# A gated mix of a state-space convolution and an MLP: the last stage's adds move from DMA to VectorE, with named PSUM banks

## The chip, the core and the metric

The kernel runs on one core of a Trainium2 chip. The metric is the device time of one execution in microseconds (us); lower is better. TensorE (PE) multiplies, with its weight loads shown apart as PEld; VectorE (DVE) and ScalarE (ACT) work on tiles; GpSimd (POOL) and SyncE (SP) mostly issue DMAs here, and so does ACT at the end. Times below are counted from the start of the profiled span unless they are called durations.

## The reference

For 2048 tokens of width 512, the output mixes two branches of the same input with a gate per token:

```python
x = A_u
g = _sigmoid((x * gate_w).sum(-1, keepdims=True))
a = _A_ref(x, ...)   # long convolution (state-space kernel K), by FFT, plus u * Dskip
b = _B_ref(x, ...)   # gelu(x @ w1 + b1) @ w2 + b2, hidden width 1792
return g * a + (1 - g) * b
```

The convolution kernel K is built from complex exponentials of 512 x 128 parameters, and the convolution over 2048 positions is done by transforms.

## The kernel before, in words

The program has two parts, `front` and `conv`. `front` runs the whole MLP branch, builds the convolution taps and does the first stage of both transforms. A planner orders its work. It ends at about 426 us and leaves in memory: `tu_d` (signal after the first stage), `tk_d` (taps after the first stage), and in the output tensor `out` the finished MLP part (1-g)·b of 14 of the 16 tiles of 128 tokens. The last two tiles (14 and 15) hold only half of their MLP sum there; the other half is added in `conv` (`rest`, L1176, 21 groups of three matmuls, and L1228).

`conv` (L1073 on) is written out in order by hand (a manual schedule: each engine runs its instructions in the order of the program). It has two stages.

**The loop of 16 steps (L1200 to L1220).** Step `s` works on two of 32 frequencies. It issues the loads that later steps need: taps tiles `tk` (L1089, two of 256 KB a step up to step 10, each first used by `taps` five steps later in numbering and about two steps later in time), matrices `cc` (L1086), and in steps 4 to 6 signal tiles (L1205). VectorE forms the complex product (`product`, L1126), PE does the next step's signal transform (`signal`, L1119, into PSUM tiles `p2u` under the tag `pu`) and the taps transform of the step after that (`taps`, L1110), then the inverse transform of the product (`inverse`, L1138, tag `pa`). `turn` (L1149) copies the two results with ScalarE into two of six staging tiles `sa` and stores each (256 KB, L1155, on SP's queue) to the scratch tensor `t4_d`, which the profile writes `t_d`. After every fourth step (3, 7, 11 and 15) the eight finished rows are fetched back by four DMAs of 512 KB (L1163) into the tiles `den` and `t3` (written `t`), turned so that the last stage can use them. I call these four DMAs a gather. The first three gathers are issued by GpSimd, the last by ScalarE. A gather waits until all stores of its four steps have landed.

After steps 12 and 13 the loop also loads two of the eight pairs of output tiles, pairs 6 and 7, from `out` into `mos[6]` and `mos[7]` (L1220, 512 KB each, SP's queue). `room` (L1167) says where a pair lies: in places of `attic` and `loft` whose signal tiles have been used by then.

**The last stage (L1223 to L1257).** Four warming matmuls (`warm`, two records each in the profile) come first. Then, for eight pairs `m` of output tiles, PE does two matmuls for each tile `pb` (L1236; in the profile each matmul is two records). A pair's two tiles are allocated together, from the tag `pu` with four buffers or, for pairs 2 and 5, the tag `pa` with two. The first matmul needs the first DMA of all four gathers (`den`). For pairs 0 to 5 VectorE scales the first tile by the gate (L1250) and ScalarE the second (L1248), and GpSimd issues a DMA of 512 KB that adds the pair to `out` in memory (L1255, `accum_op`). For pairs 6 and 7 VectorE scales and adds to the loaded `mos` tile (L1246), and plain stores follow (L1257 on SP; L1252 on SP and ScalarE, 256 KB each).

SP's queue is in order. In the built program each of its DMAs also waits for an earlier one to land: eight semaphores are used in turn, so a DMA waits for the one eight places before it.

Of the kernel before, what the change touches and what calls it, by code (L numbers as in the profile page):

```python
# [9 lines left out]
F32 = mybir.dt.float32  # L10
# [3 lines left out]
ALU = mybir.AluOpType  # L14
# [3 lines left out]
P = 128  # L18
L = 2048
D = 512  # L20
# [254 lines left out]
def gated_mix(  # L275
# [18 lines left out]
    nc = tc.nc  # L294
# [14 lines left out]
    gate = cp.tile([P, 2, 16], F32, name="gate")  # L309
# [763 lines left out]
    def conv(pool, ps, late, attic, loft, den):  # L1073
# [8 lines left out]
        def fetch(n):  # L1082
            if n % 4 == 0:
                m = n // 4
                cc = pool.tile([P, 384], F32, tag="cc", name=f"cc{m}", bufs=4)
                nc.sync.dma_start(cc, c2[m])  # L1086
                c4s[m] = cc
            t2s[n] = pool.tile([P, D], F32, tag="tk", name=f"tk{n}", bufs=N_TK)
            nc.sync.dma_start(t2s[n], tk_d[ko[n]])  # L1089
# [12 lines left out]
        def pair(s, r, c, out):  # L1102

            for i in range(2):
                n = 2 * s + i
                w = mats[n // 4][0][c][:, n % 4]
                x = t2s[n] if r else us[n]
                nc.tensor.matmul(out[64 * i : 64 * i + 64], w, x, start=True, stop=True)  # L1108

        def taps(s):  # L1110
            fac[s] = []
            for c in range(2):
                pk = ps.tile([P, D], F32, tag="pk", name=f"p2k{s}{c}", bufs=2)
                pair(s, 1, c, pk)
                k = pool.tile([P, D], F32, tag=f"k{c}", name=f"k{s}{c}", bufs=2)
                nc.scalar.copy(k, pk)  # L1116
                fac[s].append(k)

        def signal(s):  # L1119
            pus[s] = []  # L1120
            for c in range(2):
                pu = ps.tile([P, D], F32, tag="pu", name=f"p2u{s}{c}", bufs=4)
                pair(s, 0, c, pu)
                pus[s].append(pu)

        def product(s):  # L1126

            (ur, ui), (kr, ki) = pus.pop(s), fac.pop(s)
            v = [pool.tile([P, D], F32, tag=f"v{i}", name=f"v{s}{i}", bufs=2) for i in range(2)]
            nc.vector.tensor_mul(v[0], ur, kr)  # L1130
            nc.vector.tensor_mul(v[1], ur, ki)
            nc.vector.tensor_mul(zs[0], ui, ki)
            nc.vector.tensor_mul(zs[1], ui, kr)
            nc.vector.tensor_sub(v[0], v[0], zs[0])
            nc.vector.tensor_add(v[1], v[1], zs[1])
            prod[s] = v

        def inverse(s):  # L1138

            v = prod.pop(s)  # L1140
            for i in range(2):
                n = 2 * s + i
                pas[n] = ps.tile([P, D], F32, tag="pa", name=f"pa{s}{i}", bufs=2)
                r = slice(64 * i, 64 * i + 64)
                w = mats[n // 4][1][r, s % 2]
                for c in range(2):
                    nc.tensor.matmul(pas[n][64 * c : 64 * c + 64], w, v[c][r], start=True, stop=True)  # L1147

        def turn(s):  # L1149

            for n in (2 * s, 2 * s + 1):
                sa = sas[n % 6]
                nc.scalar.copy(sa, pas.pop(n))
                g, k = divmod(n, GROUP)
                nc.sync.dma_start(t4_d[g, :, k].rearrange("e c q d -> (c q) e d"), sa)  # L1155
                if k < GROUP - 1:
                    continue
                rows = t4_d[g].rearrange("e k c q d -> (e k c) q d")

                for h in range(0, 32, 8):  # L1160
                    on = nc.gpsimd if n < 31 else nc.scalar
                    to = t3[g:P:4, h - 8 : h] if h else den[g:P:4]
                    on.dma_start(to, rows[:, h : h + 8])  # L1163
# [36 lines left out]
        for s in range(16):  # L1200

            for n in range(2 * s + N_TK + (2 if s else 0), min(2 * s + N_TK + 4, 32)):
                fetch(n)
            for n in range(2 * s + N_ROOM, min(2 * s + N_ROOM + 2, 32)) if s > 3 else ():
                nc.sync.dma_start(us[n], tu_d[ko[n]])  # L1205
            product(s)
            if s + 1 < 16:
                signal(s + 1)
            if s + 2 < 16:
                if s % 2 == 0:  # L1210
                    matrices(s // 2 + 1)
                taps(s + 2)
            if s == 15:
                rest(N_REST)
            inverse(s)
            turn(s)
            if 12 <= s < 14:
                k = s - 6
                room(k)
                nc.sync.dma_start(mos[k], out[2 * k : 2 * k + 2].rearrange("s p d -> p s d"))  # L1220
        rest(14)

        warm = ps.tile([P, D], F32, tag="pa", name="warm", bufs=2)  # L1223
        for _ in range(N_KEEP):
            nc.tensor.matmul(warm[0:64], mats[7][1][:, 1], zs[0], start=True, stop=True)
        for s in range(N_LATE):
            z = mos[7][:, s]
            nc.vector.scalar_tensor_tensor(z, accs[s], gate[:, 1, 14 + s : 15 + s], z, ALU.mult, ALU.add)  # L1228

        for m in range(8):  # L1230
            tag, n = ("pa", 2) if m % 3 == 2 else ("pu", 4)
            pbs = [ps.tile([P, D], F32, tag=tag, name=f"pb{m}{i}", bufs=n) for i in range(2)]
            for i in range(2):
                for b in range(2):
                    j = 4 * m + 2 * i + b
                    nc.tensor.matmul(  # L1236
                        pbs[i][64 * b : 64 * b + 64], g1t[:, min(j, 1)], t3[:, j - 8] if j > 7 else den[:, j],
                        start=True, stop=True,
                    )
            if m < 6:  # L1240
                room(m)
            for i in range(2):
                t = 2 * m + i
                z, g = mos[m][:, i], gate[:, 0, t : t + 1]
                if m > 5:
                    nc.vector.scalar_tensor_tensor(z, pbs[i], g, z, ALU.mult, ALU.add)  # L1246
                elif i:
                    nc.scalar.mul(z, pbs[i], g)  # L1248
                else:
                    nc.vector.tensor_scalar(z, pbs[i], g, None, ALU.mult)  # L1250
                if m == 7:
                    (nc.sync, nc.scalar)[i].dma_start(out[t], z)  # L1252
            to = out[2 * m : 2 * m + 2].rearrange("s p d -> p s d")
            if m < 6:
                nc.gpsimd.dma_start(to, mos[m], accum_op=ALU.add)  # L1255
            elif m < 7:
                nc.sync.dma_start(to, mos[m])  # L1257

    ctx.enter_context(tc.manual_schedule())
    keep = ctx.enter_context(tc.tile_pool(name="keep", bufs=1))  # L1260
# [2 lines left out]
    den = keep.tile([P, N_DEN, D], F32, name="den")  # L1263
# [74 lines left out]
```

## Time and profile before

| what | value |
|---|---|
| median of 3 runs | 539.93 us (539.12 to 541.77) |
| the profiled execution's span | 539.9 us |
| PE / PEld / DVE / ACT / POOL busy | 95% / 71% / 79% / 65% / 8% |
| mean DMA rate | 194 GB/s |
| mean granted TensorE clock | 0.982 |

The span runs from the first instruction to the last, so the wait for the last stores to land lies inside it. A busy share says little here: what counts is which chain of waits ends last in `conv`, the last 113 us. In the rows of the timeline, "x8" is the count of merged instructions, and a bracket gives the idle time before them and what ended it. "SPq", "ACTq" and "PEq" are the engines' instruction queues, which issue DMAs. "DMA to landing" counts from the issue of a DMA until its data has arrived.

### The profile page before, as it was taken

To read this page: it belongs to the slowest core of one execution; us is meant where nothing else is said; L and a number is where in the kernel's file an instruction comes from. 1 tells how busy PE (TensorE), PEld (TensorE's weight loads), DVE (VectorE), ACT (ScalarE), POOL (GpSimd) and SP (SyncE) were. 2 spreads that over 40 slices of the span, in tenths; PEclk is the share of its full clock that TensorE was granted. 3 is DMA by queue.
4 is the path that set the end of the run, shared out by engine and by line. 5 is a ranking of instruction groups with operands and counts; after the bars stand their busy time and mean duration, and the time that the engine had idled before them with its cause. 6 is when DMAs were issued, how large, how long until landed. Compare 5 with 4: busy or idle time off the path is not lost.

```text
span 539.9 us, 12181 instructions
## 1 busy us (share of the span) xinstructions
PE 511.7 (95%) x4818; PEld 385.6 (71%) x4818; DVE 426.8 (79%) x806; ACT 353.5 (65%) x614; POOL 40.9 (8%) x79
## 2 busy tenths in 40 slices
PE   7878899999999999989999999999999999999981
PEld 7546789898899889777988989889888522223620
DVE  5898799999999959869999899999511388887132
ACT  4989846699875599976577987387253555555030
POOL 2000000000000000000102010101010001011040
PEclk9879999999999999999999999999999999999996
DMA  7989564162584442583887037514778758998888
GB/s 245 357 288 313 181 235 139 59 197 82 130 232 179 158 127 72 178 280 74 212 196 205 19 88 162 126 60 104 231 188 198 210 207 289 392 386 290 319 163 189
DMA packets 80837, 104.73 MB, mean 194 GB/s; under 512 B 39222, under 2 KB 43450, under 8 KB 80268
## 3 DMA queue, kind: packets, MB, share of 16 engines
q1 hardware_dynamic: 73756, 79.80, 46.7%
q0 software_dynamic: 6688, 21.79, 16.5%
q10 hardware_dynamic: 336, 2.36, 1.2%
q8 instruction: 38, 0.62, 0.4%
q14 instruction: 19, 0.16, 0.1%
HBM read 58.31 MB, written 45.62 MB: 192 GB/s over the span
## 4 chain that ended last, share of the span: by engine, by line
PE 76%; DMA 9%; ACT 8%; DVE 3%; issue 1%; SPq 1%; ACTq 0%; DVEq 0%
PE pk L681 10%; PE ph L899 8%; PE acc L947 8%; PE ph L901 8%; PE ph L900 8%; PE acc L949 7%; PE acc L948 7%; PE p2u L1108 5%; PE p2k L1108 5%; PE pa L1147 3%; PE pb L1236 3%; DMA tu_d<-attic 3%; DMA attic<-in_xs_dram 2%; PE ph L403 2%; ACT L916 1%
## 5 line engine op out<-in xcount | busy, mean ns | idle before, releaser
L899 PE MATMUL ph<-xh,wh 128*128 128x256 f32 x448 | 128.9, 288 | 3.4 <-ACT attic L421 2.2
L901 PE MATMUL ph<-xh,wl 128*128 128x256 f32 x448 | 127.6, 285 | 0.8 <-DVE wl L782 0.7
L900 PE MATMUL ph<-xlo,wh 128*128 128x256 f32 x448 | 127.2, 284 | 0.0
L899 PEld LDWEIGHTS ph<-xh,wh 128*128 128x128 f32 x448 | 85.8, 192 | 14.1 <-issue 5.6
L947 PE MATMUL acc<-wh,hh 128*128 128x512 f32 x210 | 85.1, 405 | 3.2 <-ACT hh L919 3.2
L900 PEld LDWEIGHTS ph<-xlo,wh 128*128 128x128 f32 x448 | 85.9, 192 | 2.0
L901 PEld LDWEIGHTS ph<-xh,wl 128*128 128x128 f32 x448 | 85.8, 191 | 1.6 <-DVE wl L782 1.6
L949 PE MATMUL acc<-wh,hl 128*128 128x512 f32 x210 | 83.2, 396 | 0.4 <-DVE hl L929 0.4
L948 PE MATMUL acc<-wl,hh 128*128 128x512 f32 x210 | 83.1, 396 | 0.0
L916 ACT ACTIVATE ph<-ph,b1t 128x256 f32<-128x256 f32 x112 | 50.4, 450 | 42.8 <-PE ph L901 40.8
L929 DVE TENSOR_TENSOR hl<-ph,hh 128x512 fp32r<-128x512 f32 (+1 forms) x62 | 38.5, 621 | 32.4 <-ACT hh L919 32.3
L681 PE MATMUL pk<-y,den 128*32 128x64 f32 x2048 | 61.4, 290 | 0.0
L681 PEld LDWEIGHTS pk<-y,den 128*32 128x32 f32 x2048 | 57.2, 136 | 3.7 <-issue 1.4
L947 PEld LDWEIGHTS acc<-wh,hh 128*128 128x128 f32 x210 | 39.7, 189 | 18.2 <-issue 6.8
L949 PEld LDWEIGHTS acc<-wh,hl 128*128 128x128 f32 x210 | 39.8, 190 | 11.0 <-DVE hl L929 2.1
L643 DVE TENSOR_TENSOR y<-y,ea 128x64 f32<-128x64 f32 (+4 forms) x80 | 45.5, 569 | 0.2
L948 PEld LDWEIGHTS acc<-wl,hh 128*128 128x128 f32 x210 | 39.8, 189 | 6.7
L919 ACT CAST hh<-ph 128x512 fp32r<-128x512 f32 (+1 forms) x62 | 33.0, 533 | 10.3 <-PE acc L948 6.9
L488 DVE TENSOR_TENSOR loft<-den,zz 128x256 f32<-128x256 f32 (+2 forms) x48 | 37.4, 779 | 2.7 <-ACT den L614 2.3
L489 DVE TENSOR_TENSOR loft<-den,zz 128x256 f32<-128x256 f32 (+2 forms) x48 | 37.3, 777 | 0.0
L656 DVE TENSOR_TENSOR y<-y,loft 128x2048 f32<-128x2048 f32 x16 | 36.6, 2288 | 0.0
L1116 ACT COPY k<-p2k 128x512 f32<-128x512 f32 x32 | 18.8, 586 | 25.0 <-issue 13.1
(178 smaller groups left out, 876.3 us busy)
## 6 DMA issues: line engine op xcount, KB each, us to landing
tu_d<-attic SPq DMA_DIRECT2D x64, 128.0 KB, 3.4
tk_d<-sk SPq DMA_DIRECT2D x32, 256.0 KB, 4.9
tk<-tk_d SPq DMA_DIRECT2D x32, 256.0 KB, 4.4
t_d<-sa SPq DMA_DIRECT2D x32, 256.0 KB, 4.8
t<-t_d POOLq DMA_DIRECT2D x9, 512.0 KB, 7.1
attic<-in_xt_dram SPq DMA_DIRECT2D x16, 256.0 KB, 3.8
xh_d<-xh SPq DMA_DIRECT2D x8, 512.0 KB, 3.4
xl_d<-xlo SPq DMA_DIRECT2D x8, 512.0 KB, 4.6
```

The costliest lines, as they stand in the source:

```text
L488: vec(2 * m, lambda: vv.tensor_mul(t, a, br), due, [ka, *kb], [kt])
L643: nc.vector.tensor_mul(both(n, 64 - 3 * n, n), both(0, 64 - n, n), an)
L681: nc.tensor.matmul(pks[q][32 * j : 32 * j + 32, :, gg], x[:, r, :, ch], y[:, r, :, ch], start=(r == 0), stop=(r == 1), skip_group_check=True,)
L899: nc.tensor.matmul(p, h, xh[xk][:, d], start=(d == 0), stop=False)
L900: nc.tensor.matmul(p, h, xlo[xk][:, d], start=False, stop=False)
L901: nc.tensor.matmul(p, lo, xh[xk][:, d], start=False, stop=(d == 3))
L916: nc.scalar.activation(phs[q][:, n], phs[q][:, n], AF.Gelu_apprx_tanh, bias=b1t[:, f : f + 1])
L929: nc.vector.tensor_sub(lo, phs[q][:, 0:nf], hi.bitcast(F32))
L947: nc.tensor.matmul(a, h, wh[1][w], start=start, stop=False)
L948: nc.tensor.matmul(a, h, wl[1][w], start=False, stop=False)
L949: nc.tensor.matmul(a, l, wh[1][w], start=False, stop=(j == 3))
L1108: nc.tensor.matmul(out[64 * i : 64 * i + 64], w, x, start=True, stop=True)
```

## The change

Three edits, all in `conv`.

1. PSUM tiles in the loop and the last stage get a tag of their own with one buffer each: `pu00`, `pu01`, `pu10`, `pu11` (step parity, real or imaginary) and `pa0`, `pa1`. In the last stage pair `m` takes `pu0x`, `pu1x` or `pax` by `m % 3`, and a tile is allocated just before its matmuls.
2. All eight output pairs are loaded in the loop: pair `k` after step `7 + k`, so in steps 7 to 14.
3. In the last stage VectorE does all sixteen tiles with one scale-and-add; ScalarE's scaling and GpSimd's adding DMAs are gone. Pairs 0 to 6 are stored by plain DMAs on SP's queue; pair 7 as before.

```diff
-                pu = ps.tile([P, D], F32, tag="pu", name=f"p2u{s}{c}", bufs=4)
+                pu = ps.tile([P, D], F32, tag=f"pu{s % 2}{c}", name=f"p2u{s}{c}", bufs=1)
...
-                pas[n] = ps.tile([P, D], F32, tag="pa", name=f"pa{s}{i}", bufs=2)
+                pas[n] = ps.tile([P, D], F32, tag=f"pa{i}", name=f"pa{s}{i}", bufs=1)
...
-            if 12 <= s < 14:
-                k = s - 6
+            if 7 <= s < 15:
+                k = s - 7
                 room(k)
                 nc.sync.dma_start(mos[k], out[2 * k : 2 * k + 2].rearrange("s p d -> p s d"))
...
-            tag, n = ("pa", 2) if m % 3 == 2 else ("pu", 4)
-            pbs = [ps.tile([P, D], F32, tag=tag, name=f"pb{m}{i}", bufs=n) for i in range(2)]
+            tag = "pa" if m % 3 == 2 else f"pu{m % 3}"
             for i in range(2):
+                pb = ps.tile([P, D], F32, tag=f"{tag}{i}", name=f"pb{m}{i}", bufs=1)
...
-                if m > 5:
-                    nc.vector.scalar_tensor_tensor(z, pbs[i], g, z, ALU.mult, ALU.add)
-                elif i:
-                    nc.scalar.mul(z, pbs[i], g)
-                else:
-                    nc.vector.tensor_scalar(z, pbs[i], g, None, ALU.mult)
+                z = mos[m][:, i]
+                nc.vector.scalar_tensor_tensor(z, pb, gate[:, 0, t : t + 1], z, ALU.mult, ALU.add)
                 if m == 7:
                     (nc.sync, nc.scalar)[i].dma_start(out[t], z)
-            to = out[2 * m : 2 * m + 2].rearrange("s p d -> p s d")
-            if m < 6:
-                nc.gpsimd.dma_start(to, mos[m], accum_op=ALU.add)
-            elif m < 7:
-                nc.sync.dma_start(to, mos[m])
+            if m < 7:
+                nc.sync.dma_start(out[2 * m : 2 * m + 2].rearrange("s p d -> p s d"), mos[m])
```

SP's queue before, from the stores of step 9 to those of step 11 (`t_d<-sa` are the two stores of a step, `tk` the taps tiles):

```order
L1155 DMA t_d<-sa_4776 64x2x512
L1155 DMA t_d<-sa_4777 64x2x512
L1089 DMA tk_5260<-tk_d 128x512
L1089 DMA tk_5262<-tk_d 128x512
L1155 DMA t_d<-sa_4778 64x2x512
L1155 DMA t_d<-sa_4779 64x2x512
L1155 DMA t_d<-sa_4780 64x2x512
L1155 DMA t_d<-sa_4781 64x2x512
```

and the same stretch now (`attic<-out_dram` and `loft<-out_dram` are loads of output pairs):

```order
L1155 DMA t_d<-sa_4776 64x2x512
L1155 DMA t_d<-sa_4777 64x2x512
L1220 DMA attic<-out_dram 128x2x512
L1089 DMA tk_5263<-tk_d 128x512
L1089 DMA tk_5265<-tk_d 128x512
L1155 DMA t_d<-sa_4778 64x2x512
L1155 DMA t_d<-sa_4779 64x2x512
L1220 DMA loft<-out_dram 128x2x512
L1155 DMA t_d<-sa_4780 64x2x512
L1155 DMA t_d<-sa_4781 64x2x512
```

A 512 KB load now stands ahead of each step's taps tiles and stores; pairs 0 to 3 stand ahead of the stores of step 11, the last that the third gather waits for, and pair 7 stands just ahead of the stores of step 15.

The end of SP's queue before, from the stores of step 13:

```order
L1155 DMA t_d<-sa_4778 64x2x512
L1155 DMA t_d<-sa_4779 64x2x512
L1220 DMA attic<-out_dram 128x2x512
L1155 DMA t_d<-sa_4780 64x2x512
L1155 DMA t_d<-sa_4781 64x2x512
L1155 DMA t_d<-sa_4776 64x2x512
L1155 DMA t_d<-sa_4777 64x2x512
L1257 DMA out_dram<-loft 128x2x512
L1252 DMA out_dram<-attic 128x512
```

and now, from the stores of step 14:

```order
L1155 DMA t_d<-sa_4780 64x2x512
L1155 DMA t_d<-sa_4781 64x2x512
L1220 DMA attic<-out_dram 128x2x512
L1155 DMA t_d<-sa_4776 64x2x512
L1155 DMA t_d<-sa_4777 64x2x512
L1246 DMA out_dram<-attic 128x2x512 x3
L1246 DMA out_dram<-loft 128x2x512 x4
L1244 DMA out_dram<-attic 128x512
```

The seven plain stores of the pairs have joined SP's queue; the six adding DMAs have left GpSimd's.

VectorE's queue in the last stage before, all of it:

```order
L1250 TENSOR_SCALAR attic<-pb_5509,gate 128x512
L1250 TENSOR_SCALAR attic<-pb_5518,gate 128x512
L1250 TENSOR_SCALAR attic<-pb_5527,gate 128x512
L1250 TENSOR_SCALAR loft<-pb_5536,gate 128x512
L1250 TENSOR_SCALAR loft<-pb_5545,gate 128x512
L1250 TENSOR_SCALAR loft<-pb_5554,gate 128x512
L1246 SCALAR_TENSOR_TENSOR loft<-pb_5563,gate,loft 128x512
L1246 SCALAR_TENSOR_TENSOR loft<-pb_5564,gate,loft 128x512
L1246 SCALAR_TENSOR_TENSOR attic<-pb_5572,gate,attic 128x512
L1246 SCALAR_TENSOR_TENSOR attic<-pb_5573,gate,attic 128x512
```

and now, the first eight of sixteen:

```order
L1242 SCALAR_TENSOR_TENSOR attic<-pb_5515,gate,attic 128x512
L1242 SCALAR_TENSOR_TENSOR attic<-pb_5519,gate,attic 128x512
L1242 SCALAR_TENSOR_TENSOR attic<-pb_5524,gate,attic 128x512
L1242 SCALAR_TENSOR_TENSOR attic<-pb_5528,gate,attic 128x512
L1242 SCALAR_TENSOR_TENSOR attic<-pb_5533,gate,attic 128x512
L1242 SCALAR_TENSOR_TENSOR attic<-pb_5537,gate,attic 128x512
L1242 SCALAR_TENSOR_TENSOR loft<-pb_5542,gate,loft 128x512
L1242 SCALAR_TENSOR_TENSOR loft<-pb_5546,gate,loft 128x512
```

VectorE has sixteen instructions there instead of ten. PE's order is the same in both programs.

More of the change, by code (lines that the diff above doesn't have):

```diff
@@ L1221, in conv @@
         rest(14)
-        warm = ps.tile([P, D], F32, tag="pa", name="warm", bufs=2)
+        warm = ps.tile([P, D], F32, tag="pa0", name="warm", bufs=1)
         for _ in range(N_KEEP):
@@ L1236, in conv @@
                     nc.tensor.matmul(
-                        pbs[i][64 * b : 64 * b + 64], g1t[:, min(j, 1)], t3[:, j - 8] if j > 7 else den[:, j],
+                        pb[64 * b : 64 * b + 64], g1t[:, min(j, 1)], t3[:, j - 8] if j > 7 else den[:, j],
                         start=True, stop=True,
                     )
-            if m < 6:
-                room(m)
-            for i in range(2):
                 t = 2 * m + i
-                z, g = mos[m][:, i], gate[:, 0, t : t + 1]
-                if m > 5:
-                    nc.vector.scalar_tensor_tensor(z, pbs[i], g, z, ALU.mult, ALU.add)
-                elif i:
-                    nc.scalar.mul(z, pbs[i], g)
-                else:
-                    nc.vector.tensor_scalar(z, pbs[i], g, None, ALU.mult)
+                z = mos[m][:, i]
+                nc.vector.scalar_tensor_tensor(z, pb, gate[:, 0, t : t + 1], z, ALU.mult, ALU.add)
                 if m == 7:
                     (nc.sync, nc.scalar)[i].dma_start(out[t], z)
-            to = out[2 * m : 2 * m + 2].rearrange("s p d -> p s d")
-            if m < 6:
-                nc.gpsimd.dma_start(to, mos[m], accum_op=ALU.add)
-            elif m < 7:
-                nc.sync.dma_start(to, mos[m])
+            if m < 7:
+                nc.sync.dma_start(out[2 * m : 2 * m + 2].rearrange("s p d -> p s d"), mos[m])
     ctx.enter_context(tc.manual_schedule())
```

## The prediction

> **What bounds the kernel now.** The page puts PE on 76% of the chain, but the change touches only `conv`, so I read first the chain that ended last from 485 us on (start, duration, what):
>
> ```profile
> 487.81 1.72 PE p2k L1108 x8
> ...
> 509.06 3.15 PE warm L1225 x7
> 512.26 0.37 PE warm L1225
> 512.63 6.87 PE pb L1236 x31
> 519.50 1.10 PE pb L1236 x4
> 520.63 0.76 DVE loft L1250
> 521.44 1.96 PE pb L1236 x8
> 523.42 0.76 DVE loft L1250
> 524.23 4.54 PE pb L1236 x20
> 528.79 0.75 DVE attic L1246
> ```
>
> The loop is bound by PE without a gap (the steps follow each other every 4.6 us). In the last stage the chain goes back and forth between PE and DVE from pair 4 on, and it ends at 529.54, while the span ends at 539.9. The timeline of the last stage shows the back and forth:
>
> ```profile
> 511.62 0.64 PE L1236 MATMUL pb<-den,g1t 128*64 128x512 f32 x1
> ...
> 516.98 0.75 DVE L1250 TENSOR_SCALAR attic<-pb,gate 128x512 f32<-128x512 f32 x1 [0.97 <-PE pb L1236]
> ...
> 518.70 0.75 DVE L1250 TENSOR_SCALAR loft<-pb,gate 128x512 f32<-128x512 f32 x1 [0.97 <-PE pb L1236]
> ...
> 521.44 1.94 PE L1236 MATMUL pb<-t,g1t 128*64 128x512 f32 x8 [0.85 <-DVE loft L1250]
> ...
> 527.93 1.61 DVE L1246 SCALAR_TENSOR_TENSOR attic<-pb,gate,attic 128x512 f32<-128x512 f32 x2
> 528.71 0.61 SPq L1252 DMA_DIRECT2D out_dram<-attic  x1
> ```
>
> Undisturbed, a pair takes 1.72 us (518.70 - 516.98), 0.86 a tile. But at 521.44 PE starts pair 4's second tile only when DVE has emptied pair 4's first (520.63 + 0.76): the shared tag gave both the same buffer.
>
> Then the DMAs, by stretches (the columns of use are the last two, share of the 16 engines and GB/s):
>
> ```profile
> 470.00:475.00 5.00, 5.00 (x28) 1.41 (x26) 4.08 (x7) 2.27 (x5) 0.00 (x0) 1.00 1.06 404
> ...
> 477.50:484.50 7.00, 7.00 (x38) 1.99 (x34) 5.72 (x10) 3.75 (x8) 0.55 (x2) 1.00 1.01 374
> ...
> 489.50:492.50 3.00, 3.00 (x20) 0.94 (x20) 2.06 (x5) 1.66 (x3) 1.45 (x3) 1.00 0.48 81
> 492.50:499.50 7.00, 7.00 (x39) 2.44 (x36) 6.11 (x11) 3.32 (x6) 0.59 (x2) 1.00 0.87 330
> 499.50:506.50 7.00, 7.00 (x35) 4.90 (x34) 1.22 (x2) 1.08 (x2) 0.00 (x0) 1.00 1.01 385
> 506.50:508.50 2.00, 2.00 (x11) 1.65 (x10) 0.00 (x0) 0.00 (x0) 0.00 (x0) 1.00 0.07 26
> ...
> 516.70:537.30 20.60, 10.33 (x44) 2.83 (x41) 6.01 (x8) 2.86 (x5) 5.90 (x5) 0.85 1.04 204
> ```
>
> Two readings. The tail is DMA-bound: the adding DMAs fill the engines from 516.7 to 537.3 at 204 GB/s, half the rate of plain ones. And the loop's second half has hardly any DMA time left: apart from 3 us at 490 and 2 us at 507 it runs full or nearly so, at about 400 GB/s at best. The DMA issues say what is waited for (start, duration, queue, line; a landing row answers to the issue above it):
>
> ```profile
> 476.01 0.51 POOL L1163 DMA_DIRECT2D den<-t_d  x1 [20.22 <-DMA t_d<-sa]
> ...
> 491.05 0.51 POOL L1163 DMA_DIRECT2D den<-t_d  x1 [13.00 <-DMA t_d<-sa]
> ```
> ```profile
> 478.85 1.33 SPq L1089 DMA_DIRECT2D tk<-tk_d  x2
> ```
> ```profile
> DMA to landing us min/median/max: 8.3/8.3/8.4
> ```
> ```profile
> 486.62 6.24 SPq L1155 DMA_DIRECT2D t_d<-sa  x4
> ```
> ```profile
> DMA to landing us min/median/max: 3.2/3.3/3.3
> ```
> ```profile
> 507.23 0.51 ACTq L1163 DMA_DIRECT2D den<-t_d  x1
> ```
> ```profile
> DMA to landing us min/median/max: 4.1/4.4/4.7
> ```
>
> While the second gather runs (from 477.5 for 7 us), a taps load takes 8.3 us to land: SP's queue nearly stands still. The third gather starts at 491.05, when step 11's stores have landed (issued from 486.62 on, 3.3 us); behind it SP's queue empties until 506.5 and the last stores land. Only then, at 507.23, does the fourth gather start, and 4.1 us later `pb` begins. So the start of the last stage, 511.6, hangs on a chain of DMAs: stores of step 11, third gather, flush of SP's queue, fourth gather. The four warming matmuls just cover it.
>
> **The change part by part.** *Named banks.* In the loop PE has no gap to give back: nothing. In the last stage `pb` ran from 511.62 to DVE's end at 528.79 + 0.75 = 529.54, 17.92 us. With a pair's banks used again only three pairs later, PE runs through: 8 x 1.72 = 13.76, then DVE's last 0.75 and a handover of 0.06 (521.44 against 521.38), 14.57 in all. Gain 3.35.
>
> *Sixteen scale-and-adds on DVE instead of ten instructions there and six on ACT.* Two take 1.61 us, 0.80 each, below PE's 0.86 a tile, so they hide behind PE; without that cover they would cost 16 x 0.80 = 12.9, still less. ACT is only idle earlier. DVE now waits for the loaded pairs too; they all stand ahead of step 15's stores on SP's queue, so they have landed before `pb` begins, and L1228, which waits for pair 7, is two instructions that fit into PE's wait. Behind the plain stores, which wait for DVE, nothing stands on SP's queue.
>
> *Plain stores.* Before, the stores at the end waited for the adding ones:
>
> ```profile
> out_dram<-io SPq DMA_DIRECT2D x16, 256.0 KB, 2.5
> ...
> out_dram<-attic POOLq DMA_DIRECT2D x3, 512.0 KB, 7.9
> ...
> out_dram<-attic SPq DMA_DIRECT2D x1, 256.0 KB, 8.9
> ```
>
> From DVE's end to the span's end it was 539.94 - 529.54 = 10.4: the last store landed at 537.6 (issued 528.7, 8.9 us), and 2.3 follow. The eight plain stores are 4.2 MB, 10.5 us at 400 GB/s, spread over 14 us of `pb`: no backlog but the pair just before. A store of this size landed in 2.5; I take 2.9 for the neighbour. New tail 2.9 + 2.3 + 0.1 = 5.3. Gain 5.1. Bounds: 2.5 and 4.7 us (the slowest DMA of the fourth gather, above) for the landing, so a gain of 3.3 to 5.5.
>
> *Six more loads in the loop, and two a step later.* 524 KB each, 1.3 us at 400 GB/s. Nothing waits for their data until 516, but SP's queue is in order. Pairs 0 to 3 stand ahead of step 11's stores: 4 x 1.3 = 5.2 us. These stores now land 0.8 us later than an empty queue would allow (3.3 against 2.5), so the queue holds no slack and nearly all of it counts: I take 5.0 for the third gather, 491.05 to 496.1. It still needs its 7 us, and about 2.8 us pass between the landing and its first data (the near-idle 489.5 to 492.5); these 2.8 us are now used by the queue. Behind it SP must move two loads more than before, 2.6 us, less those 2.8 and 0.3 of rounding: the last stores land 4.5 later.
>
> ```profile
> L1155 SPq DMA_DIRECT2D t_d<-sa x12: 518/540/1355, 482.0 to 502.7; - x12
> ```
>
> Their issue (502.7) is not what is late: 4 us of PE delay would hide behind the queue. So a gap of PE in the loop would not move the end. There may be one: the taps tiles that PE wants at 487.81 now stand behind pairs 0 and 1 (2.6 us) on a queue that the second gather holds up until 484.5; I count 0.6 us for it, between 0 and 3, and nothing of it in the sum. Last stage from 516.1. Bounds: 2 (a fuller use of the two lulls) and 7.8 (all six loads exposed).
>
> *The gap on PE.* `rest` and `warm` end at 512.1 as before, so PE waits about 4 us. The granted clock has shown what that does (PE busy is the second number, clock the third last):
>
> ```profile
> 15.72:19.13 3.41, 1.45 (x6) 0.82 (x6) 3.05 (x6) 3.33 (x7) 0.68 (x2) 1.00 1.04 409
> 19.13:22.54 3.41, 3.41 (x10) 2.64 (x9) 3.16 (x6) 3.35 (x11) 0.00 (x0) 0.50 1.05 362
> 520.89:524.30 3.41, 2.01 (x10) 0.56 (x12) 1.24 (x2) 0.69 (x1) 1.57 (x2) 1.00 1.08 189
> 524.30:527.72 3.42, 3.42 (x17) 1.14 (x19) 1.40 (x2) 0.69 (x1) 1.59 (x2) 1.00 1.13 201
> ```
>
> The clock changes in steps of 3.41 us; a stretch with 1.45 us of PE work was followed by one at half clock, one with 2.01 was not. Of a gap of 4 us some 2 us at least fall into one such stretch and leave it 1.4 of work, so `pb` runs half-speed for up to 3.41 us and loses up to 1.7; part of it may fall into the gap. I take 1.5 (bounds 0 and 3.4, two stretches). The Trainium skill, "TensorE: Matmul & The Clock Gate", section "Part 1: The HAM clock gate (the "warmup" mystery)", has the clock go down after an idle window of about 3.4 us; by that a gap of 4 us seldom holds a whole window, and this term would be nothing. The two rows at 15.72 and 19.13 speak against it, since that stretch was not idle.
>
> *The sum.* 539.94 - 3.35 - 5.1 + 4.5 + 1.5 = 537.5. The profiled execution (539.94) stands at the median (539.93).
>
> **The rivals.** *The loads hide.* If the lulls and the taps' lead take them up, `pb` starts at 511.6 and only the gains are left: 539.94 - 8.45 = 531.5. For it: 3 us at 81 GB/s. Against: 2.1 MB against 1 MB of lull, which comes after the bytes are due. Chance 0.10.
>
> *The clock stays full.* The delay is there, but the gap falls so, or is so short, that no stretch at half clock meets `pb`: 536.0. For it: a gap of PE in the loop would shift `warm` later and shorten the wait. Chance 0.25, for the one stretch of 1.45 is all the evidence against. The Trainium skill's page on the clock gate, named above, is on this rival's side.
>
> *The loads are exposed in full (slower).* SP's queue issues a DMA only when the one eight places before has landed. If 512 KB loads caught behind the gathers hold it up, the lulls stay empty and all six loads count: 7.8, and a wait of 7 us gives two stretches at half clock, 3.4. 539.94 - 8.45 + 11.2 = 542.7. It decides where delay and clock together pass 11.15 (the gains and 0.5%): `pb` starts at 519.4 or later. For it: SP has waited so before (row below). Against: the engines were full then, so no DMA time was lost. Chance 0.08.
>
> ```profile
> SPq L1155 <- DMA t_d<-sa: 4.9, 2, 4.2
> ```
>
> *The banks change nothing:* PE still stops for DVE, 3.35 back: 540.9. Chance 0.04; the new tags leave no choice of buffer.
>
> **How the numbers follow.** Forecast 537.5 with 0.53; its own range by the bounds is about 535 to 540. A measurement of this kernel can tell 0.5%, 2.7 us: faster means below 537.2, slower above 542.6. Faster: all of the first rival (0.10), 0.19 of the second, and 0.21 of the forecast, whose middle is just above the line: 0.50. Slower: 0.07 of the third and 0.01 from the last. The rest, 0.42, is the same. The range goes from 533.5 (the second rival with a shorter delay) to 541.0 (the banks' failure), and leaves out the first rival and the third.
>
> **What would show it.** Right: no DVE release inside PE's `pb` rows, which last 13.8 us plus a half-clock part; after DVE's end some 5.3 us; GpSimd's third gather issued about 496; ScalarE's about 511.7; a row at 0.50 near 516. Wrong: third gather at 491 to 493 (the loads hid), or `pb` beginning after 519.

## The result, and the profile after

The changed kernel took 536.04 us in the median of 10 runs (533.68 to 539.02), the kernel before 540.98 us beside it (10 runs, 539.12 to 543.01). The ratio is 0.9903 with a 95% interval from 0.9878 to 0.9928, so it is faster by about 1%, and the interval leaves out 1. The profiled execution has a span of 537.2 us and a time of 539.02, the slowest of its ten runs; before's profiled execution had a span of 539.9 and took 541.77. A time thus lies some 1.8 us above its span. This pair differs by only 2.75 us where the medians differ by 4.9, because the profiled executions lie 3.0 us (changed) and 0.8 us (before) above their medians. The start of the loop moves from one profile to the next (its first taps matmul stands at 424.46 us in the profile before, at 422.1 to 424.5 in the twelve profiles of the others), though nothing changes ahead of it. So places in `conv` are compared below as counted from that matmul ("after the loop's start").

The chain that ended last, of the changed kernel, from 487 us on (start, duration, what):

```profile
487.66 2.54 PE p2k L1108 x8
...
503.32 9.28 DMA t_d<-sa
...
512.70 4.45 DMA den<-t_d
517.15 0.14 issue
517.29 15.65 PE pb L1236 x64
532.94 0.03 issue
532.96 0.75 DVE attic L1242
```

The back and forth between PE and DVE is gone: the last stage is one row of 64 matmul records, 15.65 us without a stop, and DVE ends 0.79 us behind it. In front of it stands what was hidden before: the stores of step 15, which take 9.28 us to land, and the fourth gather's first DMA, 4.45 us. The span ends at 537.25, 3.5 us behind DVE's end, where it was 10.4.

The third gather's issue, from the timeline of GpSimd (the bracket is the wait before it and what ended it):

```profile
496.63 0.51 POOL L1163 DMA_DIRECT2D den<-t_d  x1 [18.64 <-DMA loft<-out_dram]
```

It was 491.05 before. After the loop's start that is 72.4 us instead of 66.6. The bracket names the load of an output pair, but that load (pair 4, issued at 490.90) stands behind the stores of step 11, so the gather cannot depend on it; it only shares one of the eight semaphores. What the gather waits for are the two stores of step 11 (first row: start, duration, queue; second row: their landing):

```profile
488.94 1.22 SPq L1155 DMA_DIRECT2D t_d<-sa  x2
```
```profile
DMA to landing us min/median/max: 6.3/6.4/6.4
```

Before, they were issued from 486.62 on and took 3.3 us. So after the loop's start they are issued 2.5 us later and take 3.1 us longer, which makes 5.6 of the 5.8 us. The fourth gather follows at 88.4 instead of 82.8, `pb` at 93.0 instead of 87.2: 5.9 us later. The matmuls of `pb` and the gap in front of them:

```profile
509.64 3.65 PE L1225 MATMUL warm<-z,cc 128*64 128x512 f32 x8
517.29 5.33 PE L1236 MATMUL pb<-den,g1t 128*64 128x512 f32 x16 [4.01 <-DMA den<-t_d]
522.44 10.48 PE L1236 MATMUL pb<-t,g1t 128*64 128x512 f32 x48
```

The first 16 records take 5.33 us, though the next 48 take only 10.48, 3.5 for 16. The stretches of the clock show why (PE busy second, granted clock third from the end):

```profile
510.39:513.81 3.42, 2.89 (x7) 0.69 (x5) 1.41 (x2) 0.00 (x0) 0.00 (x0) 1.00 0.28 107
513.81:517.22 3.41, 0.00 (x0) 0.00 (x0) 0.00 (x0) 0.00 (x0) 0.00 (x0) 1.00 0.97 322
517.22:520.63 3.41, 3.34 (x8) 1.12 (x10) 0.75 (x1) 0.00 (x0) 0.00 (x0) 0.51 0.69 293
520.63:524.05 3.42, 3.42 (x18) 1.25 (x16) 2.78 (x4) 0.00 (x0) 0.00 (x0) 0.99 0.41 155
```

After a stretch without any PE work `pb` runs its first 3.4 us at half clock, and takes 1.9 us more than the 13.76 of the sum. And the use of the DMA engines (last two columns) in the same parts of `conv` as before:

```profile
485.00:495.50 10.50, 10.47 (x56) 2.77 (x48) 7.80 (x14) 5.73 (x11) 0.00 (x0) 1.00 1.01 390
495.50:498.00 2.50, 2.50 (x16) 0.69 (x16) 1.58 (x3) 1.07 (x2) 1.37 (x3) 1.00 1.18 397
...
512.00:514.00 2.00, 1.28 (x3) 0.14 (x1) 0.87 (x2) 0.00 (x0) 0.00 (x0) 1.00 0.06 11
...
520.50:536.00 15.50, 12.42 (x58) 4.22 (x54) 11.26 (x15) 0.00 (x0) 0.00 (x0) 0.99 0.72 272
```

The lull ahead of the third gather's data (81 GB/s before) is filled at 397, and the tail, where the engines were saturated at 204 GB/s by adding DMAs, now moves 272 GB/s and has 28% left.

### The profile page after: what moved, and what is told of

Its sections match the earlier page's. It is cut to its first block, busy times and chain, and to the rows that moved or that the text cites. A ratio compares the mean times of both kernels' runs of the same rounds, so it can differ in the third digit from the quotient of the medians.

```text
span 537.2 us, 12201 instructions
## 1 busy us (share of the span) xinstructions
PE 514.5 (96%) x4818; PEld 387.1 (72%) x4818; DVE 431.2 (80%) x812; ACT 349.3 (65%) x608; POOL 33.7 (6%) x73
## 4 chain that ended last, share of the span: by engine, by line
PE 74%; DMA 10%; ACT 9%; DVE 2%; issue 2%; SPq 1%; ACTq 0%; DVEq 0%
PE pk L681 10%; PE ph L899 8%; PE acc L947 8%; PE ph L901 8%; PE ph L900 8%; PE acc L949 7%; PE acc L948 7%; PE p2u L1108 6%; PE p2k L1108 5%; PE pb L1236 3%; PE pa L1147 3%; PE ph L403 2%; DMA t_d<-sa 2%; ACT L916 2%; DMA tu_d<-attic 2%
## 5 line engine op out<-in xcount | busy, mean ns | idle before, releaser
L1116 ACT COPY k<-p2k 128x512 f32<-128x512 f32 x32 | 18.7, 586 | 25.9 <-issue 14.8
```

## The experiments

The theory: the gain comes from the tail (plain stores, and PE no longer stopped), the price from loads that stand on SP's queue ahead of stores that the third and the fourth gather wait for, with a half-clock stretch on top. The rivals are that the loads cost nothing, that the banks alone bring the gain, and that the total of DMA work sets the end wherever the loads stand. All places are us after the loop's start in the profile, "end" is the end of the span; ratios are to the kernel before, run beside each.

| kernel | median us | ratio (95% interval) | 3rd / 4th gather | `pb` starts | end |
|---|---|---|---|---|---|
| before | 540.98 | 1 | 66.6 / 82.8 | 87.2 | 115.5 |
| changed | 536.04 | 0.9903 (0.9878 to 0.9928) | 72.4 / 88.4 | 93.0 | 113.0 |
| loads alone | 544.56 | 1.006 (1.0027 to 1.0093) | 71.8 / 86.7 | 91.2 | 120.9 |
| banks alone | 541.0 | 0.9987 (0.996 to 1.0013) | 66.5 / 83.0 | 87.3 | 116.5 |
| no loads | 531.01 | 0.9804 (0.9766 to 0.9843) | 67.1 / 83.5 | 87.9 | 106.1 |
| longer warming | 535.42 | 0.9887 (0.9848 to 0.9927) | 71.6 / 86.7 | 91.1 | 109.8 |
| late loads | 535.68 | 0.9906 (0.9873 to 0.9939) | 67.4 / 84.8 | 90.9 | 109.2 |
| shared banks | 536.19 | 0.9905 (0.9874 to 0.9937) | 72.8 / 88.7 | 93.0 | 112.9 |
| changed, again | 536.98 | 0.9908 (0.9884 to 0.9932) | 74.0 / 89.4 | 93.8 | 113.8 |
| loads behind gather | 539.3 | 0.996 (0.9931 to 0.9989) | 66.6 / 85.2 | 89.6 | 113.7 |
| three in loop | 541.55 | 1.0013 (0.9986 to 1.004) | 66.6 / 84.0 | 88.1 | 115.9 |
| changed, beside these | 535.37 | 0.9884 (0.9843 to 0.9924) | 72.3 / 87.5 | 91.8 | 111.5 |
| loads after gather | 537.64 | 0.9944 (0.9918 to 0.9969) | 67.3 / 85.0 | 89.3 | 112.1 |

**Loads alone.** The kernel before, with all eight pairs loaded after steps 7 to 14; the data of pairs 0 to 5 is overwritten unused.

```diff
-            if 12 <= s < 14:
-                k = s - 6
+            if 7 <= s < 15:
+                k = s - 7
...
-            if m < 6:
-                room(m)
```

> The kernel before with only the loads changed: all eight pairs are loaded after steps 7 to 14, but pairs 0 to 5 are then overwritten by the scaling and added by DMA as before, so their loads serve nothing. Theory (the loads stand ahead of the stores in SP's queue and shift the chain of gathers): third gather issued near 496.6 instead of 491.05, fourth near 512.7 instead of 507.2, first pb near 517.3, and behind it the old last stage of 28.3 us plus up to 1.9 us of half clock: span 545.5 to 547.5, 1.0 to 1.4% slower than before. Rival (the loads hide in the lulls, and the later start of the last stage in the changed kernel has another cause, such as the new waits on banks): within 1 us of before.

It took 544.56 us, 0.6% more, and the profile shows the third gather 5.2 us later, `pb` 4.0 us later, half clock at its start, and the end 5.5 us later. The way of the cost is the one predicted. Its size in the medians, 3.2 us (0.6%), is less than the 1.0 to 1.4% expected and less than in the one profile. That the loads hide is ruled out.

**Banks alone.** The kernel before with the new tags only.

```diff
-                pu = ps.tile([P, D], F32, tag="pu", name=f"p2u{s}{c}", bufs=4)
+                pu = ps.tile([P, D], F32, tag=f"pu{s % 2}{c}", name=f"p2u{s}{c}", bufs=1)
...
-            tag, n = ("pa", 2) if m % 3 == 2 else ("pu", 4)
-            pbs = [ps.tile([P, D], F32, tag=tag, name=f"pb{m}{i}", bufs=n) for i in range(2)]
+            tag = "pa" if m % 3 == 2 else f"pu{m % 3}"
+            pbs = [ps.tile([P, D], F32, tag=f"{tag}{i}", name=f"pb{m}{i}", bufs=1) for i in range(2)]
...
```

> The kernel before with only the PSUM tags changed. Theory A (the tail is bound by the adding DMAs, which fill the DMA engines from 516.7 on): PE runs pb through in 13.8 us and ends 3.3 us earlier, but the last store lands at most 0.7 us earlier; span 539.2 to 539.9. Theory B (the term of the prediction's sum stands by itself): 3.35 us less, span 536.6.

The chain shows PE running through. Its row of 13.76 us holds 61 of the 64 records; the first three overlap those of `warm`. The page shows the adding DMAs of pairs 3 to 5 (size, median us to landing):

```profile
511.62 13.76 PE pb L1236 x61
525.38 0.03 issue
525.40 0.75 DVE attic L1246
```
```profile
out_dram<-loft POOLq DMA_DIRECT2D x3, 512.0 KB, 12.7
```

DVE ends 2.4 us earlier after the loop's start (3.3 were expected), yet the time is the same (0.9987). These adding DMAs are issued earlier and take longer to land (12.7 us here, 9.2 before); the engines stay full at 201 GB/s, against 204. A wait on PE was removed where DMA set the end.

**No loads.** The changed kernel without the loads of pairs 0 to 5, so that the MLP part is missing from twelve output tiles.

```diff
             if 7 <= s < 15:
                 k = s - 7
                 room(k)
+                if k < 6:
+                    continue
                 nc.sync.dma_start(mos[k], out[2 * k : 2 * k + 2].rearrange("s p d -> p s d"))
```

> The changed kernel without the loads of pairs 0 to 5: VectorE adds whatever lies in the rooms of these pairs, so the MLP part is missing from twelve output tiles; all other work stands. Theory (the six loads delay the start of the last stage): third gather near 491, pb from 511.6 without half clock, 14.6 us to VectorE's end and 3.5 us behind it: span 529.5 to 530.5, 7 us below the changed kernel's profile. Rival (the loads hide): pb starts at 517 as in the changed kernel, span 536 to 537.

The end of its chain on PE (start, duration, what):

```profile
508.21 3.58 PE warm L1227 x8
511.79 13.77 PE pb L1238 x63
```

It took 531.01 us. Both gathers are back near their old places, PE goes from warming to `pb` without a gap, and `pb` takes 13.77. So the first and the third edit together are worth 10.4 us (541.38 beside it), and the six loads cost some 5 of these (531.01 against the 536.04 above, which was measured on another occasion).

**Longer warming.** The changed kernel with eight warming matmuls instead of four, to fill the gap.

```diff
-N_KEEP = 4
+N_KEEP = 8
```

> The changed kernel with eight warming matmuls in place of four, so that PE has work until about 516.5. Theory (the wait for the fourth gather halves the clock at the start of pb): no stretch at half clock there, pb 13.8 instead of 15.65 us, span 535.3 against 537.2 of the changed kernel's profile, and since how much of the half-clock stretch meets pb depends on the clock's phase, the runs should also spread less than the 5 us of the changed kernel. Rival (the half clock is rare and was met by chance in the profiled run): no change of the median, 536.

The same two rows of its chain:

```profile
506.82 6.58 PE warm L1225 x15
513.40 14.19 PE pb L1236 x63
```

There is no gap, and no half clock: `pb` runs in 14.2 us instead of 15.65. In the medians, though, it is only 0.6 us below the changed kernel's (535.42 and 536.04), less than the intervals can tell, and its eight runs spread over 5.1 us, no less than the ten of the changed kernel (5.3). The profiled execution (533.69) lay 1.7 us below its median, so the early end in the table is not all due to the clock. That the half clock was there and that warming removes it is shown; that it costs the time of a typical run 1.5 us is not.

**Late loads.** The same eight loads, all behind the stores that the third gather waits for: pairs 0, 1, 2 and 7 after steps 11 to 14, pairs 3 to 6 on SP's queue behind the stores of step 15 (`fill` does `room` and the load).

```diff
...
+                for q in range(3, 7) if s == 15 else ():
+                    fill(q)
...
-            if 7 <= s < 15:
-                k = s - 7
-                room(k)
-                nc.sync.dma_start(mos[k], out[2 * k : 2 * k + 2].rearrange("s p d -> p s d"))
+            if 11 <= s < 15:
+                fill((0, 1, 2, 7)[s - 11])
```

> The changed kernel with the same eight loads at other places in SP's queue: pairs 0, 1, 2 and 7 after steps 11 to 14, pairs 3 to 6 behind the stores of step 15. No load stands ahead of the stores of step 11, and only four ahead of those of step 15, two of which fit into the lull at the third gather. Theory (what counts is what stands ahead of the stores that a gather waits for): counted from the first matmul of the loop, third gather at 66.6 us as in the kernel before (72.4 in the changed one), fourth at 82.8 to 84 (86.7 to 88.4), pb from 87.2 to 88.3 on without half clock, end of the span at 106 to 107.5 as without loads; time 531 to 532.5, ratio to before 0.981 to 0.984. Rival (the loads cost DMA time wherever they stand): span and time as the changed kernel, 535 to 536, ratio 0.990.

Its chain from the fourth gather on:

```profile
508.03 5.97 DMA den<-t_d
514.00 0.14 issue
514.13 13.97 PE pb L1242 x64
```

The third gather is back (67.4), so the place of the first four loads on the queue is what had moved it. But the fourth gather's first DMA now takes 5.97 us, since the loads of pairs 3 to 6 move at the same time (it is 4.29 again in the kernel with loads behind the gather, below), and `pb` starts only 1 to 3 us earlier than in the three profiles of the changed kernel. The profile ends 2.3 to 4.5 us earlier than those, but it shows the fastest of its seven executions; in the medians there is nothing (0.9906, and 0.9908 for the changed kernel beside it). The expected ratio was missed.

**Shared banks.** The changed kernel with the old tags: `pu` with four buffers, `pa` with two, a pair allocated together.

```diff
...
-            tag = "pa" if m % 3 == 2 else f"pu{m % 3}"
+            tag, n = ("pa", 2) if m % 3 == 2 else ("pu", 4)
+            pbs = [ps.tile([P, D], F32, tag=tag, name=f"pb{m}{i}", bufs=n) for i in range(2)]
             for i in range(2):
-                pb = ps.tile([P, D], F32, tag=f"{tag}{i}", name=f"pb{m}{i}", bufs=1)
+                pb = pbs[i]
```

> The changed kernel with the old shared PSUM tags: loads, sixteen scale-and-adds and plain stores stay. Theory (once the tail is no longer bound by the adding DMAs, what PE loses by shared banks is paid in full): PE waits for DVE from pair 3 or 4 on, about 0.85 us for each tile in turn, so pb takes 3 to 8 us longer and the kernel too: time 539 to 543 against 535.4 to 536. Rival (the banks never matter, the stores and loads do all): time within 1 us of the changed kernel.

PE's rows of the last stage, from its timeline (the bracket is the wait and what ended it):

```profile
516.29 5.28 PE L1237 MATMUL pb<-den,g1t 128*64 128x512 f32 x16 [3.62 <-DMA den<-t_d]
521.39 10.48 PE L1237 MATMUL pb<-t,g1t 128*64 128x512 f32 x48
```

No row of `pb` waits for DVE, and the 48 records take 10.48 us as with named banks; the time is the same (0.9905). In the built program of the kernel before, both tiles of pair 4 lie in one bank, and both of pair 5 in another; in this one, with the same tags, every pair has two banks and PE comes back to a bank only three pairs later. That the tiles are now emptied by one engine in their order is the likely reason for the better choice. The named banks are worth nothing in this kernel.

**The changed kernel again**, beside the last two.

> The changed kernel once more, unchanged, for a second profile and more runs on the chip of the other two. If the half-clock stretch at the start of pb is the rule, this profile shows it too and the loop's first matmul to the span's end takes 112 to 113 us; if it was chance, 110 to 111. The time up to the loop's first matmul should differ from run to run by 1 to 2 us and explain most of the spread.

Ratio 0.9908, with half clock at the start of `pb` as in the first profile; the end lies 113.8 us after the loop's start instead of 113.0, so a difference of 1 us between two single profiles says nothing. The expected 112 to 113 us were missed, and the start of the loop does not explain most of the spread: over the three profiles of the changed kernel it moves by 1.8 us, what comes behind it by 2.3.

**Loads behind the gather.** As late loads, but pairs 3 to 6 go to ScalarE's queue, behind the DMAs of the fourth gather in turn.

```diff
...
-                for q in range(3, 7) if s == 15 else ():
-                    fill(q)
...
                     on.dma_start(to, rows[:, h : h + 8])
+                    for q in ((), (3,), (4, 5), (6,))[h // 8] if s == 15 else ():
+                        fill(q, nc.scalar)
```

> The changed kernel, with the loads of pairs 0, 1, 2 and 7 on SP's queue after steps 11 to 14 (behind the stores that the third gather waits for), and those of pairs 3 to 6 on ScalarE's queue between the DMAs of the fourth gather, behind its first one: first, second, pair 3, third, pairs 4 and 5, fourth, pair 6. Theory A (a load costs what it delays of the stores and of the fourth gather's first DMA, and nothing behind it): the third gather is issued 66.5 to 67.5 us after the loop's first taps matmul, as before the change, the fourth at 83.5 to 85, its first DMA takes 4.0 to 4.7 us (it was 5.97 with the same loads on SP's queue beside it), pb starts 87.7 to 89.5 after that matmul, without a stretch at half clock, and the span ends 106 to 108.5 after it; ratio 0.979 to 0.986, 2 to 6 us below the changed kernel. Theory B (the amount of DMA work behind step 11 sets the end, wherever the loads stand): the first DMA of the fourth gather, or VectorE's wait for pairs 3 to 6, takes back what the third gather gains; PE's pb rows show stops released by VectorE, pb lasts over 15 us, and the ratio is 0.988 to 0.993, as for the changed kernel.

The chain of the last stage:

```profile
507.92 4.29 DMA den<-t_d
...
512.35 1.95 PE pb L1241 x8
514.30 0.03 issue
514.32 0.76 DVE attic L1247
515.09 0.02 issue
515.10 6.02 DMA out_dram<-attic
521.12 0.02 issue
521.14 5.59 DMA t<-t_d
...
526.87 5.37 PE pb L1241 x16
```

The first half went as theory A has it, or within 0.2 us of it: the fourth gather's first DMA is back at 4.29 us and `pb` starts 2 to 4 us earlier than in the changed kernel. Then something that neither theory held: the fourth DMA of the gather, on ScalarE's queue, is issued at 521.14, when pair 0's plain store, on SP's queue, has landed (issued 515.10, 6.02 us). The eight semaphores go round over both queues, and in the built program's order that store is eight places before it. PE stops for 4.0 us and then runs at half clock. The median is 539.3 us, a ratio of 0.996, outside what either theory expected.

**Three in the loop.** As the one before, with the load of pair 2 moved from the loop to the place of pair 3's.

```diff
-                    for q in ((), (3,), (4, 5), (6,))[h // 8] if s == 15 else ():
+                    for q in ((), (2, 3), (4, 5), (6,))[h // 8] if s == 15 else ():
...
-            if 11 <= s < 15:
-                fill((0, 1, 2, 7)[s - 11])
+            if 12 <= s < 15:
+                fill((0, 1, 7)[s - 12])
```

> As the kernel with loads behind the gather, but only pairs 0, 1 and 7 are loaded in the loop (after steps 12 to 14), and pair 2 goes with pair 3 behind the second DMA of the fourth gather. Theory A: one load of 1.3 us less stands ahead of step 15's stores, so the fourth gather is issued 0.5 to 1.3 us earlier than there, at 83 to 84 us after the loop's first taps matmul; VectorE may wait up to 1 us for pair 2; ratio 0.977 to 0.986. Theory B: no difference from the changed kernel (0.988 to 0.993).

The last long pieces of its chain:

```profile
517.07 6.21 DMA out_dram<-attic
523.31 6.59 DMA t<-t_d
530.04 6.38 PE pb L1241 x16
```

The fourth gather comes 1.2 us earlier (84.0), as theory A had it, but now the gather's last DMA waits for the store of pair 1, and PE stops for 6.8 us. The median is 541.55 us, and nothing is left of the gain. The changed kernel, run beside both:

> The changed kernel as it is, beside these two on the same chip: ratio 0.988 to 0.993 by both theories, so that the two can be held against it directly. pb starts 92 to 93.5 us after the loop's first taps matmul and meets a stretch at half clock.

Its ratio is 0.9884, with half clock from 514.2 us on and `pb` starting at 91.8, just before the expected 92.

**Loads after the gather.** As loads behind the gather, but the four DMAs of the fourth gather stand together on ScalarE's queue, and the loads of pairs 3 to 6 behind them.

```diff
-                    for q in ((), (3,), (4, 5), (6,))[h // 8] if s == 15 else ():
+                    for q in ((), (), (), (3, 4, 5, 6))[h // 8] if s == 15 else ():
```

> As the kernel with loads behind the gather, but the four DMAs of the fourth gather stand together on ScalarE's queue and the loads of pairs 3 to 6 all behind them. There, the last gather DMA waited on that queue until a plain store of pair 0 had landed, so PE stopped for 4 us in the middle of pb. Theory A (the stop came from the place of that DMA in the round of eight semaphores, not from the loads' bytes): pb again starts 87.7 to 90 us after the loop's first taps matmul, PE has no stop for a gather DMA, VectorE may wait up to 2 us for pair 6, no stretch at half clock falls into pb, and the span ends 106.5 to 109.5 after that matmul; ratio 0.980 to 0.987. Theory B (what the loads move behind step 11 has to be paid, wherever they stand): the later DMAs of the gather and the loads still come too late for PE and VectorE, the span ends 111 or later after that matmul, ratio 0.988 to 0.996.

Its chain in the last stage:

```profile
512.10 1.95 PE pb L1241 x8
...
514.07 0.76 DVE attic L1247
...
514.85 8.20 DMA out_dram<-attic
...
523.15 4.14 DMA loft<-out_dram
```

PE's stop is gone, so its cause was the place of that DMA in the round of semaphores. But the wait has moved on: pair 6's load is issued when pair 0's store has landed, 8.20 us after its issue (the gather and the other loads keep the engines 95% busy from 510 to 520 us), and VectorE waits 3.9 us for the load. DVE ends at 530.1, and the ratio of 0.9944 is worse than the changed kernel's. By the numbers theory B is right for this kernel, and by the chain it is the same wait on a store's semaphore as in the two before, not the bytes alone. No order of the loads that was run beats the changed kernel in the medians. Whether another order, with five loads in the loop for instance, would keep part of the 5 us is open.

## Why the prediction was right, and where not

- **What bounds the kernel.** Both readings held. The tail was DMA-bound: removing PE's stops alone brought nothing (banks alone). And the loop's second half had little DMA time to spare: the loads moved both gathers.
- **Named banks, 3.35 us.** PE does run through, and from `pb`'s first record to DVE's end the kernel without loads takes 14.8 us (the sum had 14.57). But the credit stands in the wrong place: named banks without plain stores gave 0.9987 and moved DVE's end by 2.4 us, all of which the adding DMAs took back; plain stores on shared banks gave 0.9905, the whole change 0.9884 to 0.9908. The third edit ends PE's stops without the first, and it is also what lets their end count.
- **Plain stores, 5.1 us.** Mis-sized. The tail is 3.5 us, not 5.3, so this term is 6.9. The landing was right (2.60 us for the last 256 KB on SP's queue; I took 2.9). The 2.3 us "that follow" the last landing were copied from a tail of adding DMAs. There GpSimd's closing DRAIN, an instruction behind its adding DMAs, runs for 12.8 us from 526.3 on and ends at 539.1, 1.5 us after the last landing, and the other engines' closing instructions come behind it. In the changed kernel, without adding DMAs, this DRAIN is over by 508.5; in the kernel without loads the last store lands at 528.75 and the span ends at 529.72, 1.0 later.
- **Six more loads, 4.5 us.** Step by step right: third gather 496.63 (I said 496.1), fourth 512.70 (511.7), `pb` at 517.29 (516.1). After the loop's start `pb` is 5.9 us later in this profile, 6.6 and 4.6 in the two others of the changed kernel, so the term is some 5.7, inside the bounds of 2 to 7.8. What was too small is the delay of the third gather: 5.0 counted, 5.8 measured here, 7.4 and 5.7 in the two others. Behind it I had counted 0.5 won back (two more loads against the lull); it was 0.1 here, 0.8 and 0.9 in the others.
- **PE's stall at the taps, 0.6 us, not in the sum.** The row of 2.54 us instead of 1.72 shows 0.8, and the end did not move by it, since `pb` waits for DMAs.
- **The clock, 1.5 us.** The half-clock stretch came in all three profiles of the changed kernel and cost `pb` 1.6 to 1.9 us there. Its price in the medians is not shown (longer warming). The working was weaker than I wrote: the stretch with 1.45 us was not all the evidence, for in the same profile one with 2.13 us was followed by half clock too (rows in the last section), more than the 2.01 that I took for enough.
- **The sum.** In profiles after the loop's start: start of `pb` +5.9, `pb` to DVE's end 16.4 instead of 17.9, -1.5, tail -6.9, together -2.5; the sum had +4.5, -1.85 and -5.1, together -2.4. Two errors, 1.4 late at the start of `pb` and 1.8 early in the tail, nearly cancelled; that was luck. The median fell by 4.9 instead, twice the sum. The profiled execution was the slowest of its ten, and one kernel's end after the loop's start differs by 2.3 us over three profiles. I also took the span for the execution's time, 1.8 us too little: by its own terms the sum gives 539.3 for a profiled execution, which was 539.02, and 537.5 only against the median, which was 536.04. So the direction, the mechanism and the range held. The value is 1.5 us off, and the tail is the likely reason: the third profile of the changed kernel (changed, beside these) lies 0.8 us above its median, as the one before does, and there the start of `pb` is +4.6, `pb` to DVE's end -1.8 and the tail -6.9, together -4.0. Against the sum only the tail is far off.
- **The rivals.** That the loads hide fell (third gather at 496.6, not 491 to 493). "The clock stays full" named 536.0, which the median hit, but its mechanism did not happen: half clock stands in the profiles, and the missing 1.5 us came from the tail instead, so the hit is chance. That the loads are exposed in full fell: `pb` started before 519. That the banks change nothing happened in a way I had not thought of: they do nothing, and PE does not stop for DVE all the same.

## What to carry to other kernels

Before a wait on a compute engine is counted as gain, find out what ends last behind it: here PE's stops were real, and removing them alone was worth nothing under saturated DMA engines. When adding DMAs are replaced by loads, an add and plain stores, the bytes move into an earlier stage: count them against that stage's queue, by what stands behind each load and who waits for that, and look for the next DMAs that share its semaphores. The DMA that a bracket names need not be the one that was waited for, when several share a semaphore. A single profile of each kernel told the places to within some two microseconds but not the gain: 2.5 us in the profiles, 4.9 in the medians.

## What the runs showed of the hardware

The granted clock falls after stretches that were far from idle. In the changed kernel's run beside the others (same columns as above):

```profile
510.80:514.21 3.41, 1.05 (x3) 0.14 (x1) 0.00 (x0) 0.00 (x0) 0.00 (x0) 1.00 0.77 235
514.21:517.62 3.41, 2.91 (x8) 1.11 (x10) 0.75 (x1) 0.00 (x0) 0.00 (x0) 0.50 0.90 375
```

and in late loads:

```profile
512.52:515.93 3.41, 1.79 (x10) 0.80 (x12) 0.68 (x1) 0.00 (x0) 0.00 (x0) 1.00 1.04 434
515.93:519.35 3.42, 3.42 (x20) 1.37 (x18) 2.99 (x5) 0.00 (x0) 0.00 (x0) 1.00 0.76 299
```

PE waited for its data almost equally long (2.86 us and 2.77 us), but in the first kernel the stretch held 1.05 us of work and the next ran at half clock, while in the second the wait fell over the edge of two stretches with 2.25 and 1.79 us, and the clock stayed full. PE's busy time in a stretch does not decide it alone, though. In the profile before:

```profile
29.37:32.78 3.41, 2.13 (x12) 0.40 (x12) 3.28 (x11) 3.12 (x4) 0.00 (x0) 1.00 0.92 297
32.78:36.20 3.42, 1.97 (x4) 0.29 (x4) 3.42 (x7) 3.42 (x5) 0.00 (x0) 0.50 0.98 270
```

In the second profile of the changed kernel (changed, again) even a stretch with 2.63 us, from 42.00 us on, was followed by half clock. Over the thirteen profiles every full-clock stretch with less than 1.6 us of PE work was followed by half clock and none with more than 2.7 us was; in between both happened, and what decides there is not shown. The Trainium skill, "TensorE: Matmul & The Clock Gate", section "Part 1: The HAM clock gate (the "warmup" mystery)", names an idle window of about 3.4 us as the condition; the profile of the changed kernel would fit that (a stretch with 0.00), the rows with 1.05 and 2.13 do not.

Plain stores of 512 KB land in 2.8 to 3.9 us in the changed kernel's tail; the ones on the chains of the three kernels with loads behind or after the gather took 6.0 to 8.2 us; and of the adding DMAs the last three took a median of 9.2 us before and 12.7 us with PE running through. And in these programs, where the DMAs of two queues take their semaphores from one round of eight, a DMA on one queue waited for a store on the other: PE stood for 4.0 and 6.8 us in two kernels.
